# A 32-head softmax attention beside a linear attention on one core: the offset copies of the score tiles made by GpSimd alone, four tiles at a time

## The chip, the core and the metric

One core of a Trainium2 chip. Five engines run their own instruction lists and meet at semaphores: TensorE (PE), VectorE (DVE), ScalarE (ACT), GpSimd (POOL) and SyncE (SP, which issues most transfers). The metric is the device time of one execution in microseconds, the median of several.

## The reference

Two attention blocks over x of 2048 x 512, each with 32 heads of 16, side by side in the output. Block A is linear attention (cheap), block B is full softmax attention and sets the size of the work.

```python
def _A_ref(x, wqkv, wo):            # q, k, v: 32 heads of 16
    phi = lambda t: jnp.where(t > 0, t + 1, jnp.exp(t)) + 1e-6
    pq, pk = phi(q), phi(k)
    kv = jnp.einsum("bhsd,bhse->bhde", pk, v)
    z = jnp.einsum("bhsd->bhd", pk)
    num = jnp.einsum("bhqd,bhde->bhqe", pq, kv)
    den = jnp.einsum("bhqd,bhd->bhq", pq, z)[..., None] + 1e-6
    ...                             # num / den, heads joined, @ wo
def _B_ref(x, wqkv, wo):
    scores = jnp.einsum("bhqd,bhkd->bhqk", q, k) * scale
    p = _softmax(scores, axis=-1)
    o = jnp.einsum("bhqk,bhkd->bhqd", p, v)
    ...                             # heads joined, @ wo
return jnp.concatenate([a, b], axis=-1)
```

## The kernel before

**The work.** Block B is cut into 32 units (`NU`): four groups of eight heads, four stretches of 512 queries, and even or odd heads of the group. A unit has 64 score tiles of 128 keys x 512 queries, four heads side by side in the four row groups of the PE array, so there are 2048 score tiles in all. The scores come scaled by `ESC`, so that an exponential in base two can be made from their bits.

**Two ways to the exponential.** Some score tiles go to ACT: one exponential over two or three PSUM banks (line 1095, written to `PT`). The others, called D tiles here, go to DVE: it adds a constant and writes the sum as a 16-bit integer (line 970, `DI`), whose bits are read as a half-precision number, a rough exponential. To smooth it, two more copies of `DI` with 341 and 683 added to the integers are made (line 1166, `DJ`; these are the shifts), and all three are multiplied with V, scaled by 1, 0.797 and 0.633 (`VV`, with `SW`). So an ACT tile costs one product with V, a D tile three. The products (line 1224) add up in one PSUM bank (`pPV`), four row groups at once.

**PSUM.** Eight banks: one for `pPV`, five for ACT's tiles in two slots of three and two banks (`ABL = (3, 2)`, tensor `pS`), two for D tiles and for the projections and block A (`pD`). The third bank of slot 0 can be lent to the D side; the ACT fill is then two banks wide.

**Groups and rings.** D tiles are gathered in groups of `DG = 3` in one of `NDG = 6` buffers of `DI`; a full group is shifted twice, each time into the next of `NDJ = 8` buffers of `DJ`. A buffer of `DJ` is free again when PE has used its tiles. A unit's end: DVE transposes `pPV` to `OT` (line 1354), inverts the sums (`ZRA`), POOL multiplies (`XN`, line 1359), DVE transposes back to `ON`. POOL makes the scaled copies of V too (line 671), but the first eight are made by DVE.

**What sets the order.** A planner in the kernel's own code walks a model of the four engines with a duration for each instruction and picks, at each step, the candidate that can start first, with priorities. The order that it finds is fixed for each engine; on the chip the engines only wait for each other's semaphores, and each list runs strictly in order. `want_lend` (line 984) decides whether slot 0 is filled with two or three banks; `d_pick` (913) lets a new D tile in while the modelled backlogs of DVE and POOL are below `DBL` and `PBL`; `shift_cand` (1148) chooses between POOL and DVE for each shift (`LM` is how much later POOL must be before DVE is taken); `pv_cand` (1181) places the products, with a higher priority once `VHI` of them are outstanding; `fill_idle` puts matmuls without a use into idle PE time, by the share of PE time that was streamed lately. `SEEDS` shifts the due times of block A's and the projections' jobs.

Of the kernel before, what the change touches and what calls it, by code (L numbers as in the profile page):

```python
# [13 lines left out]
ALU = mybir.AluOpType  # L14
# [3 lines left out]
class _Op:  # L18
    __slots__ = ("idx", "lane", "fn", "pos", "waits", "sig", "count", "vc",
                 "name", "queue")  # L20


class Sched:
    ENGINES = ("pe", "act", "dve", "pool")

    def __init__(self):
        self.ops = []
        self.lane_ops = defaultdict(list)
        self.queue_ops = defaultdict(list)
        self.last_write = {}  # L30
        self.readers = defaultdict(list)
        self.clock = defaultdict(dict)
        self.acc_tag = {}
        self.n_dma_lanes = 0

# [4 lines left out]
    def add(self, lane, fn, reads=(), writes=(), name="", queue=None,  # L40
            extra_deps=(), accum=None, force_signal=False):
        if queue is None:
            queue = lane
            assert lane in self.ENGINES, lane
        op = _Op()
# [7 lines left out]
        op.sig = force_signal  # L53
        op.count = 0
# [188 lines left out]
def bass_concat_heads__linear_attn_block__softmax_full_mha__prompt_kernel(nc, A_x, A_wqkv, A_wo, B_x, B_wqkv, B_wo, out):  # L243
# [11 lines left out]
    DG = 3  # L255
    NDG = 6
    NDJ = 8
    UB = NT * 4
    PVB = 8
    PVW = 0.3  # L260
# [4 lines left out]
    LD = 1  # L265
    LB = 99.0
    PB5 = 3.0
# [3 lines left out]
    DLEAD = 0.8  # L271
    DBL = 4.0
    PBL = 7.5
    SHL = ("pool", "pool")
    LM = 5.0
    FU = 0.6
    SEEDS = (0, 195, 365, 131, 7, 89, 76, 286, 0, 222, 34, 197, 397, 382, 371)
    SEG = 45.0
    JIT = 6.0
    LATE = 0.2  # L280
    DBAL = 1
    CPRIO = 0.9
    VHI = 24
    LONE = 0.0
    XNT = 0.63
# [6 lines left out]
    JU = 0.55  # L292
# [18 lines left out]
    with es:  # L311
# [51 lines left out]
        DBANK = [bank(DB, i, ("D", i)) for i in range(ND)] + [bank(SCT, aoff[0] + ABL[0] - 1, ("S", 0, ABL[0] - 1))]  # L363
# [95 lines left out]

        def vis(eng, en_):  # L460
# [19 lines left out]
        class Job:  # L480
# [8 lines left out]
            def start_time(self):  # L489
# [3 lines left out]
                if T["pe"] >= rd - AE and streaming(T["pe"]) < JU:  # L493
# [19 lines left out]
            def go(self, i, end, bk, bi):  # L513
# [4 lines left out]
                push(eng2, end if eng2 == eng else vis(eng, end),  # L518
# [41 lines left out]
        def first_units():  # L560
            def mm(bk, kind, c0, n, o0):
                def f(e):
                    for cc in range(4):
                        ins = mm4(e, bk[0][:, bk[2] + o0:bk[2] + o0 + n], Wb[:, cc, kind * 512:kind * 512 + 128], xTb[:, cc, c0:c0 + n], cc == 0, cc == 3)
# [9 lines left out]
            mm(ka, 1, 0, 128, 0)  # L574
            mm(DBANK[0], 0, 0, 256, 0)
            mm(DBANK[1], 0, 256, 256, 0)
            mm(kb, 1, 128, 384, 0)
            km(ka, 0, 0, 128, kma_keys(0))
            qt(DBANK[0], "act", 0)
            qt(DBANK[1], "dve", 256)  # L580
# [68 lines left out]
        def v4_job(t4, Gp, lane="pool", **kw):  # L649
# [14 lines left out]
            for k in (1, 2):  # L664
                if VVP == 1 and lane == "dve":
# [5 lines left out]
                st.append((lane, 0.74 if lane == "dve" else VVT, f_op(lane, lambda e, k=k: e.tensor_scalar(  # L671
                    vv(k), vv(0), SW[k], 0.0, op0=ALU.mult, op1=ALU.add),
                    [("VV", t, sl, 0) for t in ts] + [("VV1", sl)], [("VV", t, sl, k) for t in ts])))
# [202 lines left out]
        dfree = [0.0] * ND + [None]  # L876
        held = {}
        lent = [False]
# [34 lines left out]
        def d_pick(at, used):  # L913

            bi = min((i for i in range(ND + 1) if dfree[i] is not None), key=lambda i: (dfree[i], i), default=None)
# [727 lines left out]
```

## Time and profile before

| | us |
|---|---|
| median of 3 runs | 683.81 (683.69 to 686.09) |
| the profiled execution | 684.12 |
| its span, first to last instruction | 682.4 |
| busy: ACT / PE / POOL / DVE | 669.0 / 653.9 / 622.1 / 582.6 |

The profiled execution lies 0.31 us above the median, and 1.72 us of it lie outside the span. In the rows, a group reads: line, engine, operation, what is written from what, shape, count, then busy time and the mean of one in ns, then the engine's idle time before them and what ended it. Lines that run on one engine without a gap overlap in their latencies, so the pace of a run of equal instructions (its length less one, over their number less one) says more than the mean of one. A clock of 1.00 is TensorE at full speed.

### The profile page before, as it was taken

What the parts mean: (1) busy time and instruction counts of PE and PEld (TensorE: products, weight loads), DVE (VectorE), ACT (ScalarE), POOL (GpSimd) and SP (SyncE); (2) the same over time, 40 slices, a digit from 0 to 9 for tenths busy, and PEclk for the clock granted to TensorE, in tenths of its full rate; (3) what the DMA queues carried; (4) which work ended last, traced back from release to release, by engine and by line L of the source; (5) the groups of instructions that cost most, each with busy time, mean ns of one, the idle gap of its engine ahead of it and who ended that gap; (6) DMA issues with size and microseconds to landing.
All of it is one profiled execution on the core that took longest, in us unless ns stands there. A gap on an engine that the chain in (4) does not pass through costs nothing.

```text
span 682.4 us, 19594 instructions
## 1 busy us (share of the span) xinstructions
PE 653.9 (96%) x8530; PEld 209.9 (31%) x8530; DVE 582.6 (85%) x937; ACT 669.0 (98%) x706; POOL 622.1 (91%) x470
## 2 busy tenths in 40 slices
PE   8999999999999999999999999999999999999997
PEld 4323333222323333332322233222332222322223
DVE  5878898999789988868999898888888998898983
ACT  5999999999999999999999999999999999999997
POOL 6698999999699999999999999999999999999894
PEclk9999999999999999999999998999999999999999
DMA  9400012011101201130111000111010110001111
GB/s 207 103 2 2 17 16 35 10 31 23 34 2 33 33 17 17 22 82 11 24 25 33 24 18 18 24 47 25 18 36 13 33 32 25 9 17 33 47 41 35
DMA packets 55418, 21.76 MB, mean 32 GB/s; under 512 B 45600, under 2 KB 55328, under 8 KB 55328
## 3 DMA queue, kind: packets, MB, share of 16 engines
q1 hardware_dynamic: 54128, 20.07, 13.4%
q8 instruction: 68, 1.11, 0.7%
q10 hardware_dynamic: 1200, 0.39, 0.2%
q14 instruction: 22, 0.18, 0.1%
HBM read 4.19 MB, written 4.19 MB: 12 GB/s over the span
## 4 chain that ended last, share of the span: by engine, by line
ACT 87%; POOL 7%; PE 3%; DVE 2%; DMA 1%; issue 0%; ACTq 0%
ACT PT L1095 85%; POOL DJ L1166 6%; ACT pD L683 1%; DVE DI L970 1%; PE pS L863 1%; DMA xTb<-in_B_x_dram 1%; ACT pS L683 1%; PE pD L535 1%; PE pPV L1224 1%; PE pS L535 1%; PE pS L654 0%; POOL XN L1359 0%; ACT KV L539 0%; POOL VV L671 0%; DVE DJ L1166 0%
## 5 line engine op out<-in xcount | busy, mean ns | idle before, releaser
L1095 ACT ACTIVATE PT<-pS 128x1024 f16<-128x1024 f32 (+1 forms) x666 | 660.5, 1353 | 2.6 <-PE pS L863 1.8
L1166 POOL TENSOR_SCALAR DJ<-DI 128x1536 int16<-128x1536 int16 (+1 forms) x391 | 579.5, 1483 | 48.0 <-DVE DI L970 21.6
L970 DVE TENSOR_SCALAR DI<-pD 128x512 uint16<-128x512 f32 (+1 forms) x456 | 315.2, 705 | 48.4 <-PE pD L863 42.8
L863 PE MATMUL pS<-QT,KM 32*128 32x512 bf16 x1573 | 261.5, 385 | 21.3 <-ACT PT L1095 15.0
L1224 PE MATMUL pPV<-PT,VV 128*17 128x512 f16 (+1 forms) x1420 | 244.0, 378 | 0.5 <-DVE OT L1354 0.5
L1224 PE MATMUL pPV<-DJ,VV 128*17 128x512 f16 (+1 forms) x1256 | 231.9, 379 | 0.7 <-POOL DJ L1166 0.5
L863 PE MATMUL pD<-QT,KM 32*128 32x512 bf16 x475 | 168.5, 385 | 0.3 <-DVE PQT L684 0.3
L863 PEld LDWEIGHTS pS<-QT,KM 32*128 32x128 bf16 x1573 | 64.3, 91 | 278.0 <-ACT PT L1095 260.3
L1224 PE MATMUL pPV<-DI,VV 128*17 128x512 f16 (+1 forms) x628 | 148.3, 379 | 0.5 <-DVE OT L1354 0.4
L970 DVE TENSOR_SCALAR DI<-pS 128x512 uint16<-128x512 f32 x153 | 104.1, 681 | 8.0 <-PE pS L863 4.4
L1224 PEld LDWEIGHTS pPV<-PT,VV 128*17 128x17 bf16 x1420 | 49.8, 88 | 44.0 <-issue 38.1
L1224 PEld LDWEIGHTS pPV<-DJ,VV 128*17 128x17 bf16 x1256 | 47.9, 88 | 47.2 <-issue 35.6
L863 PEld LDWEIGHTS pD<-QT,KM 32*128 32x128 bf16 x475 | 39.7, 91 | 9.3 <-issue 4.1
L1224 PEld LDWEIGHTS pPV<-DI,VV 128*17 128x17 bf16 x628 | 31.2, 88 | 22.4 <-issue 18.4
L1166 DVE TENSOR_SCALAR DJ<-DI 128x1536 int16<-128x1536 int16 x29 | 28.3, 977 | 0.0
L535 PE MATMUL pD<-xTb,Wb 128*32 128x512 bf16 (+1 forms) x368 | 26.7, 379 | 0.0
L535 PE MATMUL pD<-Wa,xTa 128*32 128x256 bf16 x672 | 26.4, 275 | 0.0
L1354 DVE STREAM_TRANSPOSE OT<-pPV 128x512 f32<-128x512 f32 x31 | 22.0, 708 | 0.7 <-PE pPV L1224 0.6
L1359 POOL TENSOR_TENSOR XN<-OT,ZRA 128x256 bf16<-128x256 f32 x31 | 19.5, 630 | 1.2
L683 ACT ACTIVATE pD<-pD 128x512 f32<-128x512 f32 x22 | 19.6, 893 | 0.0
L671 POOL TENSOR_SCALAR VV<-VV 128x544 bf16<-128x544 bf16 x24 | 17.3, 723 | 0.9
L535 PEld LDWEIGHTS pD<-Wa,xTa 128*32 128x32 bf16 x672 | 15.4, 96 | 8.7 <-issue 5.4
(109 smaller groups left out, 392.3 us busy)
## 6 DMA issues: line engine op xcount, KB each, us to landing
out_dram<-KV SPq DMA_DIRECT2D x31, 128.0 KB, 1.7
Wa<-in_A_wqkv_dram SPq DMA_DIRECT2D x3, 512.0 KB, 4.2
KM<-KR SPq DMA_DIRECT2D x96, 16.0 KB, 1.8
Wb<-in_B_wqkv_dram SPq DMA_DIRECT2D x2, 384.0 KB, 4.6
Wb<-in_B_wqkv_dram SPq DMA_DIRECT2D x1, 512.0 KB, 4.4
Wa<-in_A_wo_dram SPq DMA_DIRECT2D x1, 512.0 KB, 4.5
Wb<-in_B_wo_dram SPq DMA_DIRECT2D x1, 512.0 KB, 3.8
xTa<-in_A_x_dram SPq DMA_TRANSPOSE x24, 3.4
```

Source lines behind the costliest of these rows:

```text
L535: ins = e.matmul(out[32 * g:32 * g + 32], lhsT=lhsT[:, 32 * g:32 * g + 32], rhs=rhs, start=start, stop=stop, tile_position=(0, 32 * g))
L671: st.append((lane, 0.74 if lane == "dve" else VVT, f_op(lane, lambda e, k=k: e.tensor_scalar(vv(k), vv(0), SW[k], 0.0, op0=ALU.mult, op1=A ...
L683: ex = lambda bk: sch.add("act", lambda e: e.activation(x(bk), x(bk), ACTF.Exp), reads=[bk[3]], writes=[bk[3]])
L863: return e.matmul(dst, lhsT=KM[32 * g:32 * g + 32, Gp % 2, e_, j * 128:(j + 1) * 128], rhs=QT[32 * g:32 * g + 32, Gp % 2, c * 512:(c + 1) ...
L970: sch.add("dve", lambda e: e.tensor_scalar(DI.bitcast(U16)[:, buf, i * 512:(i + n) * 512], f32v(DBANK[bi], 512 * n), EB, IMAX, op0=ALU.add ...
L1095: sch.add("act", lambda e: e.activation(PT[:, row, c0:c0 + w], SCR[sl][:, 0:w], ACTF.Exp, scale=SC / ESC), reads=skeys(sl)[:len(bl)], writ ...
L1166: sch.add(ln, lambda e: e.tensor_scalar(J, I, 1.0, float(SH[k]), op0=ALU.mult, op1=ALU.add), reads=[("DI", buf, i) for i in range(n)], wri ...
L1224: sch.add("pe", lambda e: e.matmul(dst[32 * g:32 * g + 17, 0:n], lhsT=VV[:, Gp % 2, k, j, 17 * h:17 * h + 17], rhs=P[:, q0:q0 + n], start= ...
L1354: sch.add("dve", lambda e: e.transpose(OT[:, 0, :], PVb[:, 0:512]), reads=[("PV", g) for g in range(4)], writes=[("OT", 0)])
L1359: mul = f_op("pool" if XNP else "dve", lambda e: e.tensor_tensor(xn[:, :, 16 * e_:16 * e_ + 16], o[:, :, 0:16], zr.unsqueeze(2).broadcast_ ...
```

## The change

It touches the planner's numbers and some of its rules; the arithmetic of a tile stays.

- A group has four D tiles (`DG = 4`), in four `DI` buffers (`NDG = 4`) and six `DJ` buffers (`NDJ = 6`). A shift covers 128 x 2048.
- `LM = 99` keeps every shift on POOL. DVE's eight copies of V stay, but POOL's next instruction now waits for each of them (`hold`).
- `LD = 2` gives `want_lend` another rule: slot 0 is filled with two banks when jobs hold more D-side banks than are lent; with three when a D-side bank is free; else with two if a job is due or the backlogs are small. With `LDA` the rule also runs over the end of a unit.
- Five sets of planner constants (`MODES`) take turns by stretches of 45 us, chosen by `SEEDS`; jobs on POOL are modelled 0.8 us later (`JM`).
- The first projections are whole 128-wide matmuls instead of four 32-wide ones each.

```diff
-    DG = 3
-    NDG = 6
-    NDJ = 8
+    DG = 4
+    NDG = 4
+    NDJ = 6
...
-    LD = 1
-    LB = 99.0
-    PB5 = 3.0
+    LD = 2
+    LB = 2.0
+    PB5 = 9.0
...
-    LM = 5.0
+    LM = 99.0
...
-    SEEDS = (0, 195, 365, 131, 7, 89, 76, 286, 0, 222, 34, 197, 397, 382, 371)
+    SEEDS = (0, 2, 96, 277, 222, 0, 142, 42, 2, 142, 131, 32, 289, 309, 14)
...
-    VHI = 24
...
+    MODES = ((0.8, 36, 0.7, 0.2, 9.0), (1.2, 36, 0.7, 0.2, 9.0), (0.8, 48, 0.9, 0.2, 10.5), (1.2, 28, 0.7, 0.1, 9.0), (1.0, 36, 0.55, 0.35, 8.0))
+    LDA = 1
+    JM = 0.8
...
@@ Sched.add
+        if lane == "pool" and self.hold:
+            extra_deps = list(extra_deps) + self.hold
+            self.hold = []
...
@@ first_units
-                        ins = mm4(e, bk[0][:, bk[2] + o0:bk[2] + o0 + n], Wb[:, cc, kind * 512:kind * 512 + 128], xTb[:, cc, c0:c0 + n], cc == 0, cc == 3)
+                        ins = e.matmul(bk[0][:, bk[2]:bk[2] + n], lhsT=Wb[:, cc, kind * 512:kind * 512 + 128], rhs=xTb[:, cc, c0:c0 + n], start=(cc == 0), stop=(cc == 3))
...
@@ v4_job
+                if lane == "dve":
+                    def alone(bk, cp=cp):
+                        sch.hold.append(cp(bk))
+                        sch.hold[-1].x = 0.27
...
@@ d_pick
-            if bi is None or u is None or dfree[bi] > at or d_backlog(at) > DBL or p_backlog(at) > PBL or lagging(at):
+            if bi is None or u is None or dfree[bi] > at or d_backlog(at) > DBL or p_backlog(at) > mode()[4] or lagging(at):
...
@@ want_lend
-            if LD == 3:
+            if LD == 1:
                 return nh >= 1
...
+            free = sum(1 for x in dfree if x is not None and x <= t_ + 0.1)
+            if LD == 2 and sum(1 for i in range(len(dfree)) if held.get(i)) > sum(lent):
+                return True
+            if free:
                 return False
-            if nh >= 1 and LD != 2:
-                return True
...
-            return False
+            return d_backlog(t_) <= LB and p_backlog(t_) <= PB5
...
@@ shift_cand
-            dp, dd = POOLT(w), 0.40 + w * 0.0003
+            dp, dd = POOLT(w), DSH + max(0.0, T["pool"] - sd)
...
@@ pv_cand
-            pr = 1 if out_ >= VHI or final else 4
+            pr = 1 if out_ >= mode()[1] or final else 4
```

Three places show how the order moves. The names are those of the words above; a row is one run of equal instructions, in the order of the engine.

POOL from its first shift. Before:

```order
L1166 TENSOR_SCALAR DJ<-DI 128x1536 x14
L1359 TENSOR_TENSOR XN<-OT,ZRA 128x16x16
L1166 TENSOR_SCALAR DJ<-DI 128x1536 x11
L1359 TENSOR_TENSOR XN<-OT,ZRA 128x16x16
L1166 TENSOR_SCALAR DJ<-DI 128x1536 x6
L671 TENSOR_SCALAR VV<-VV 128x544 x4
```

POOL from its first shift, now:

```order
L1184 TENSOR_SCALAR DJ<-DI 128x2048 x10
L1379 TENSOR_TENSOR XN<-OT,ZRA 128x16x16
L1184 TENSOR_SCALAR DJ<-DI 128x2048 x8
L681 TENSOR_SCALAR VV<-VV 128x544 x5
L1184 TENSOR_SCALAR DJ<-DI 128x2048 x2
L1379 TENSOR_TENSOR XN<-OT,ZRA 128x16x16
```

Fewer and wider shifts stand between the ends of two units, and in the first units nearly as many tiles as before (40 shifted tiles instead of 42 up to the first `XN`, 40 instead of 33 up to the second).

PE from the first projections. Before:

```order
L535 MATMUL pS<-xTb,Wb 32x128 x16
L535 MATMUL pD<-xTb,Wb 32x256 x32
L535 MATMUL pS<-xTb,Wb 32x384 x16
L863 MATMUL pS<-QT,KM 128x512 x2
L535 MATMUL pD<-xTb,Wb 32x512 x16
L863 MATMUL pS<-QT,KM 128x512 x5
```

PE from the first projections, now:

```order
L573 MATMUL pS<-xTb,Wb 128x128 x4
L573 MATMUL pD<-xTb,Wb 128x256 x8
L573 MATMUL pS<-xTb,Wb 128x384 x4
L544 MATMUL pD<-xTb,Wb 32x512 x8
L881 MATMUL pS<-QT,KM 128x512 x2
L881 MATMUL pD<-QT,KM 128x512
L881 MATMUL pS<-QT,KM 128x512
L544 MATMUL pD<-xTb,Wb 32x512 x8
L881 MATMUL pS<-QT,KM 128x512 x4
```

The projection of the second stretch of keys, which stood in one piece behind the first score fill, now stands half ahead of it and half behind it, and two D tiles follow the first fill.

DVE at the end, from the last unit's first transpose. Before:

```order
L1288 STREAM_TRANSPOSE OT<-pPV 128x256
L1289 RECIPROCAL ZRA<-OT 128x8
L1288 STREAM_TRANSPOSE OT<-pD 128x256
L1289 RECIPROCAL ZRA<-OT 128x8
L1292 STREAM_TRANSPOSE ON<-XN 128x256
L1290 TENSOR_TENSOR XN<-OT,ZRA 128x8x16
L1292 STREAM_TRANSPOSE ON<-XN 128x256
L621 TENSOR_REDUCE ZRA<-ZRA 128x1 x2
L634 TENSOR_SCALAR BN<-ZRA 128x1
L635 SCALAR_TENSOR_TENSOR BN<-ZRA,BN 128x1
```

DVE at the end, now:

```order
L1309 STREAM_TRANSPOSE OT<-pPV 128x256
L1309 STREAM_TRANSPOSE OT<-pD 128x256
L1310 RECIPROCAL ZRA<-OT 128x8 x2
L1311 TENSOR_TENSOR XN<-OT,ZRA 128x8x16
L1313 STREAM_TRANSPOSE ON<-XN 128x256
L631 TENSOR_REDUCE ZRA<-ZRA 128x1 x2
L644 TENSOR_SCALAR BN<-ZRA 128x1
L645 SCALAR_TENSOR_TENSOR BN<-ZRA,BN 128x1
L1313 STREAM_TRANSPOSE ON<-XN 128x256
```

The second half of the last unit's queries now goes first, and the four small instructions of the range flag (`BN`) stand ahead of the other half's transpose to `ON`, which waits for POOL's `XN`.

Over the whole program: 314 shifts instead of 420 (391 on POOL and 29 on DVE before), 626 D tiles instead of 628, of which 125 instead of 153 in the lent bank, and ACT's exponentials are 519 of two banks and 127 of three instead of 579 and 86. Of the shifts on POOL, 88 name PE among what they wait for, instead of 27.

112 lines of the change are left out of this document (61 added, 51 removed).

## The prediction

> **What bounds the kernel now.** I read the page's busy shares and its chain first, then the groups by shape, then ACT and POOL in order of time, the clock in short stretches, and the tail.
>
> ```profile
> PE 653.9 (96%) x8530; PEld 209.9 (31%) x8530; DVE 582.6 (85%) x937; ACT 669.0 (98%) x706; POOL 622.1 (91%) x470
> ACT 87%; POOL 7%; PE 3%; DVE 2%; DMA 1%; issue 0%; ACTq 0%
> ```
>
> ACT is busy 98% of the span and carries 87% of the chain. ACT in order of time shows how little it stands still:
>
> ```profile
> 8.83 1.02 ACT L1095 ACTIVATE PT<-pS 128x1024 f16<-128x1024 f32 x1 [1.00 <-PE pS L863]
> 10.41 57.89 ACT L1095 ACTIVATE PT<-pS 128x1024 f16<-128x1024 f32 x56 [0.56 <-PE pS L863]
> ...
> 408.79 2.86 ACT L1095 ACTIVATE PT<-pS 128x1024 f16<-128x1024 f32 x3 [0.26 <-PE pS L863]
> ...
> 418.94 1.02 ACT L1095 ACTIVATE PT<-pS 128x1024 f16<-128x1024 f32 x1 [0.37 <-PE pD L863]
> 420.41 64.86 ACT L1095 ACTIVATE PT<-pS 128x1024 f16<-128x1024 f32 x65 [0.45 <-PE pD L863]
> ...
> 674.48 1.51 ACT L1016 ACTIVATE PT<-pS 128x768 f16<-128x768 f32 x2
> ```
>
> From its first exponential at 8.83 to the last one's end at 675.99 it waits only 0.56 us at the start and 0.26 + 0.37 + 0.45 = 1.08 us around 410 to 420. Behind it come 6.4 us of tail. So no order of these instructions can win more than about 1.6 us on ACT, unless ACT gets less to do.
>
> Where the 1.08 us come from, the chain and the clock tell:
>
> ```profile
> 347.11 1.47 POOL DJ L1166
> ...
> 406.29 1.48 POOL DJ L1166
> ```
>
> ```profile
> 414.00:416.00 2.00, 1.42 (x21) 0.72 (x20) 1.09 (x2) 2.00 (x3) 1.92 (x2) 1.00 0.00 0
> 416.00:418.00 2.00, 2.00 (x20) 0.89 (x19) 1.97 (x5) 2.00 (x3) 1.92 (x2) 0.70 0.00 0
> 418.00:420.00 2.00, 2.00 (x18) 1.07 (x15) 1.22 (x3) 1.59 (x2) 1.85 (x2) 0.50 0.00 0
> ```
>
> From 347 to 408 the chain runs mostly through POOL's shifts: POOL sets the pace there. Then PE is busy 1.42 us of 2 (first figure behind the length), its granted clock (third from the right) falls to 0.70 and 0.50, and ACT (fourth busy figure) loses 0.41 us in the last stretch. A late POOL is thus what already costs this kernel its only stall in the middle.
>
> The groups by shape that the change touches, and POOL's and DVE's shifts with shortest, middle and longest:
>
> ```profile
> L1166 POOL TENSOR_SCALAR DJ<-DI 128x1536 int16<-128x1536 int16 x389 | 578.2, 1488 | 47.8 <-DVE DI L970 21.6
> L1095 ACT ACTIVATE PT<-pS 128x1024 f16<-128x1024 f32 x579 | 574.9, 1299 | 2.6 <-PE pS L863 1.8 <-PE pD L863 0.8
> L970 DVE TENSOR_SCALAR DI<-pD 128x512 uint16<-128x512 f32 x437 | 292.1, 683 | 44.5 <-PE pD L863 38.9 <-PE pS L863 2.2
> L1095 ACT ACTIVATE PT<-pS 128x1536 f16<-128x1536 f32 x86 | 148.2, 1723 | 0.0
> L1166 DVE TENSOR_SCALAR DJ<-DI 128x1536 int16<-128x1536 int16 x29 | 28.3, 977 | 0.0
> L970 DVE TENSOR_SCALAR DI<-pD 128x1024 uint16<-128x1024 f32 x19 | 23.1, 1217 | 3.9 <-PE pD L863 3.9
> L1166 POOL TENSOR_SCALAR DJ<-DI 128x512 int16<-128x512 int16 x2 | 1.2, 618 | 0.2
> ```
>
> ```profile
> L1166 POOL TENSOR_SCALAR DJ<-DI x391: 618/1472/1893, 13.1 to 671.4; 128x1536 int16<-128x1536 int16 x195, 128x512 int16<-128x512 int16 x1
> ...
> L1166 DVE TENSOR_SCALAR DJ<-DI x29: 543/894/1598, 64.9 to 621.4; 128x1536 int16<-128x1536 int16 x29
> ```
>
> **The change part by part.** *ACT's work.* A two-bank exponential takes 0.92 us of ACT where they run densely (row below); one of three banks costs 1723 - 1299 = 424 ns more, 1.34. So 60 fewer of two and 41 more of three are -55.2 + 55.1, and one half-filled one goes: about -0.5 us. The last bank is not lent more but less (125 D tiles in it instead of 153), and that decides nothing by itself. Bound by ACT, the kernel can lose its 1.08 us and no more.
>
> ```profile
> 342.42 2.76 ACT PT L1095 x3
> ```
>
> *POOL's work* is the term that decides. POOL in order of time gives the pace of a shift and of what stands between:
>
> ```profile
> 339.36 15.42 POOL L1166 TENSOR_SCALAR DJ<-DI 128x1536 int16<-128x1536 int16 x10
> ...
> 38.34 1.47 POOL L1166 TENSOR_SCALAR DJ<-DI 128x1536 int16<-128x1536 int16 x1
> 39.78 0.62 POOL L1359 TENSOR_TENSOR XN<-OT,ZRA 128x256 bf16<-128x256 f32 x1
> 40.47 1.47 POOL L1166 TENSOR_SCALAR DJ<-DI 128x1536 int16<-128x1536 int16 x1
> ...
> 68.65 2.57 POOL L671 TENSOR_SCALAR VV<-VV 128x544 bf16<-128x544 bf16 x4
> ...
> 669.89 3.02 POOL L1166 TENSOR_SCALAR DJ<-DI 128x1536 int16<-128x1536 int16 x2 [0.21 <-DVE DI L970]
> ```
>
> ```profile
> L1359 POOL TENSOR_TENSOR XN<-OT,ZRA x31: 618/621/919, 39.8 to 662.5; 128x256 bf16<-128x256 f32 x31
> ```
>
> A shift of three tiles has a pace of (15.42 - 1.47) / 9 = 1.55 us. One of four isn't in the trace: by the line through 618 ns for one tile and 1472 for three, each further tile takes 427 ns, so 1.90 and with the same 0.08 between two, 1.98. The 618 rests on two instructions; if a lone tile took 0.70, the line would give 1.94; if nothing of a shift were fixed, 1.55 x 4/3 = 2.07. I take 1.98. An `XN` adds 40.47 - 38.34 - 1.55 = 0.58, a copy of V 2.57 / 4 = 0.64.
>
> Between the first and the last `XN` POOL now has 298 wide shifts, 30 `XN` and 24 copies: 590.0 + 17.4 + 15.4 = 622.8 us. Before, that stretch took 662.5 - 39.8 = 622.7 us, with 370 shifts x 1.55 + 32.8 = 606 us of work in it; the rest were waits and slowed shifts. So POOL, which had 16 us to spare, has none: it must not stand still once from 40 to 662 us to keep the pace of ACT. Behind the last `XN` it has 0.58 + 4 x 1.98 + 2 x 1.13 = 10.8 us, so its last shift ends at 39.8 + 622.8 + 10.8 = 673.4 at best. Before, it ended at 669.89 + 3.02 = 672.9, and its last products ran at 675.24 (row below), 2.3 us later. So 1.8 us of idle time in POOL are free; each further one moves the end.
>
> How much idle? Before, POOL waited 21.6 us for D tiles:
>
> ```profile
> POOL DJ L1166 <- DVE DI L970: 21.6, 16, 5.0
> ...
> 20.09 6.26 POOL L1166 TENSOR_SCALAR DJ<-DI 128x1536 int16<-128x1536 int16 x4 [0.85 <-DVE DI L970]
> 28.54 3.16 POOL L1166 TENSOR_SCALAR DJ<-DI 128x1536 int16<-128x1536 int16 x2 [2.19 <-DVE DI L970]
> 33.71 6.11 POOL L1166 TENSOR_SCALAR DJ<-DI 128x1536 int16<-128x1536 int16 x4 [2.00 <-DVE DI L970]
> ```
>
> 5.0 + 0.85 + 2.19 + 2.00 of them lie before 40 us, where the first `XN` waits for its unit anyway, so some 11.5 us lie behind. The planner now lets D tiles in until POOL is 9 instead of 7.5 us behind, and DVE has fewer other things to do, so less is left: between 0 and 11.5 I take a quarter, 3 us. That is 1.2 us beyond what is free.
>
> *DVE* loses 29 shifts (28.3 us) and gains 28 x 0.683 - 14 x 1.217 = 2.1 us for wide conversions taken apart. It has 2% of the chain: nothing on the path. *The shared way of the two.* POOL's shifts average 1488 against a middle of 1472: 389 x 16 ns = 6.2 us lost, which go with DVE's shifts; the 1.98 above is already free of them. The Trainium skill's page "SBUF — State Buffer" (section "SBUF: two separate sides") says that GpSimd and certain VectorE instructions hold a port pair for a whole instruction while the other blocks. By it 29 shifts of at least 543 ns would have cost POOL up to 15.7 us instead of 6.2; the sum takes the rows. *The eight `hold` waits* stand by the order ahead of the first `XN`, where POOL waits for D tiles already: 0. *PE* has the same score fills, four products fewer: 0. *SP's transfers* are the same and cost 1% of the chain: 0.
>
> *The start.* The projection that delayed the second exponential by 0.56 now stands half ahead of the first fill:
>
> ```profile
> 8.39 0.09 PEld L863 LDWEIGHTS pS<-QT,KM 32*128 32x128 bf16 x2 [0.32 <-DVE QT L571]
> ...
> 8.72 1.05 PE L535 MATMUL pD<-xTb,Wb 128*32 128x512 bf16 x16
> ```
>
> Its half, 0.53 us, fits partly into the 0.32 us that PE waits there. Between -0.56 and +0.5 I take -0.3 for ACT; where POOL sets the end it is worth nothing.
>
> *The tail.* DVE's end now runs the flag's small instructions ahead of the last transpose:
>
> ```profile
> 675.24 0.28 PE L1224 MATMUL pPV<-DJ,VV 128*17 128x256 f16 x2
> ...
> 677.87 0.45 DVE L1292 STREAM_TRANSPOSE ON<-XN 128x256 bf16<-128x256 bf16 x1
> 678.23 0.20 DVE L621 TENSOR_REDUCE ZRA<-ZRA 128x1 f32<-128x17 f32 x2
> ...
> 678.59 0.16 DVE L635 SCALAR_TENSOR_TENSOR BN<-ZRA,BN 128x1 f32<-128x1 f32 x1
> ```
>
> From 678.23 to 678.75 is 0.52 us, after which the last two output tiles follow: +0.6, between 0 and 1.
>
> Sum: 682.4 + 1.2 + 0.6 = 684.2 of span; 1.72 outside it make 685.9 against the profiled 684.12. The median lies 0.31 below that execution: **685.6**, 0.3% more than 683.81. By a measurement of this kernel, under 0.5% (3.4 us) can't be told from no change.
>
> **The rivals.** *A, POOL's growth is hidden.* POOL idles less than 1.8 us and ACT keeps the end, without the stall at 410 to 420: 682.4 - 1.1 - 0.5 - 0.3 + 0.6 = 681.1, at the median's level 682.5. For it: the deeper backlog and six `DJ` buffers of four tiles, as many tiles as eight of three. Against it: any 1% on a shift is 5.9 us.
>
> *B, the forecast*, POOL paces: 684 to 687.2 with 1.5 to 4.5 us of idle time.
>
> *C, slower: late shifts thin out PE's stream.* The place is wherever POOL falls behind, as at 414 us. One such event cost 1.08 us. POOL is now at its limit through all 32 units, not in one stretch of 60 us; two events on top of the forecast carry it past 687.2, four give 685.6 + 4.3 = 689.9. For it: more shifts wait for PE to empty a `DJ` buffer, the ring of which turns in 6 x 1.98 = 11.9 us instead of 12.4, and POOL's idle time there adds up. Against: in the trace of before POOL waits for PE nowhere. The Trainium skill's page "GPSIMD Engine Reference" (section 4.1, "Engine selection") speaks against the change in the same sense: elementwise work belongs on VectorE. The trace bears that out for one shift, 543 ns on DVE undisturbed against 1472.
>
> *D, faster by over 0.5%*: under 680.4 ACT would have to do less or start sooner than its rows allow.
>
> **How the numbers follow.** A 0.27, B 0.41, C 0.29, D 0.03. A and nearly all of B lie within 0.5%, with 0.05 of B above: faster 0.03, same 0.63, slower 0.34. The range reaches from A's middle into C, 682 to 692 (five events and an error of 1% in the shift); B's own is 684 to 687.2.
>
> **What would show it.** Shifts at 1.90 us with 0.08 between; POOL busy over 94% and its last shift's end between 673 and 677; POOL's share of the chain well over 7%; ACT's idle time near 3 us, in a few places behind PE's products that wait for `DJ`; the first exponentials without a gap of 0.5; the last `ON` behind the flag's rows. The prediction falls if a wide shift isn't near 1.98, if POOL waits long for PE or DVE, or if the clock drops repeatedly.

## The result, and the profile after

The changed kernel takes 686.99 us (median; 685.83 to 689.0), the kernel before beside it 684.14: a ratio of 1.0038, interval 1.0027 to 1.005. That lies in the range forecast (682 to 692), 1.4 us above the forecast of 685.6, and within the half per cent under which the prediction saw no change. The interval lies above 1 all the same: the changed kernel is the slower one, by about 0.4%. The forecast's sum, though, put the time in the wrong place.

The profiled execution has a span of 685.1 us against 682.4. The busy shares and the chain of the changed kernel:

```profile
PE 649.2 (95%) x8481; PEld 212.3 (31%) x8481; DVE 560.6 (82%) x920; ACT 668.5 (98%) x686; POOL 635.8 (93%) x393
ACT 82%; PE 10%; POOL 5%; DMA 1%; issue 0%; DVE 0%; ACTq 0%
```

POOL works longer and carries *less* of the chain (5% instead of 7%), PE 10% instead of 3%. POOL's share is a weak sign, since it varies with the execution: 0 to 6% in six traces of the changed lists, 7 to 15% in four of the lists of before (most of them come below). The groups by shape that the change touches:

```profile
L1184 POOL TENSOR_SCALAR DJ<-DI 128x2048 int16<-128x2048 int16 x312 | 593.1, 1901 | 36.7 <-DVE DI L988 12.3 <-DVE VV L681 2.1
L1111 ACT ACTIVATE PT<-pS 128x1024 f16<-128x1024 f32 x519 | 530.1, 1263 | 3.7 <-PE pS L881 1.9 <-PE pD L881 1.6
L1111 ACT ACTIVATE PT<-pS 128x1536 f16<-128x1536 f32 x127 | 212.9, 1677 | 0.5 <-PE pS L881 0.5
```

A wide shift takes 1901 ns, and POOL's list in order of time gives the pace, (5.86 - 1.90) / 2 = 1.98:

```profile
658.61 5.86 POOL L1184 TENSOR_SCALAR DJ<-DI 128x2048 int16<-128x2048 int16 x3
```

ACT in order of time, every place where it stands still and its end:

```profile
8.93 16.19 ACT L1111 ACTIVATE PT<-pS 128x1024 f16<-128x1024 f32 x17 [1.60 <-PE pS L881]
25.39 9.27 ACT L1111 ACTIVATE PT<-pS 128x1024 f16<-128x1024 f32 x10 [0.28 <-PE pS L881]
35.48 14.71 ACT L1111 ACTIVATE PT<-pS 128x1024 f16<-128x1024 f32 x15 [0.82 <-PE pD L881]
...
533.62 5.54 ACT L1111 ACTIVATE PT<-pS 128x1024 f16<-128x1024 f32 x5 [0.28 <-PE pD L881]
...
562.62 1.02 ACT L1111 ACTIVATE PT<-pS 128x1024 f16<-128x1024 f32 x1 [0.48 <-PE pD L881]
564.14 110.95 ACT L1111 ACTIVATE PT<-pS 128x1536 f16<-128x1536 f32 x108 [0.49 <-PE pS L881]
674.67 1.83 ACT L1031 ACTIVATE PT<-pS 128x768 f16<-128x768 f32 x2
679.25 0.60 ACT L548 ACTIVATE KV<-pS 128x512 bf16<-128x512 f32 x1 [2.76 <-PE pS L544]
679.88 0.39 ACTq L1333 DMA_DIRECT2D out_dram<-KV  x1
680.37 0.60 ACT L548 ACTIVATE KV<-pD 128x512 bf16<-128x512 f32 x1 [0.52 <-PE pS L544]
680.87 0.59 ACT L548 ACTIVATE KV<-pS 128x512 bf16<-128x512 f32 x1
```

The first row is the start, the last five the tail. Cut at the first exponential and at the last one's end, the two executions compare like this:

| us | before | after |
|---|---|---|
| first exponential starts | 8.83 | 8.93 |
| from there to the last one's end | 667.16 | 667.57 |
| of it, ACT stands still | 1.64 | 2.35 |
| behind the last exponential | 6.4 | 8.6 |

So 2.2 of the 2.7 us lie behind the last exponential. In the middle the gap of 0.56 us at the start is gone, as expected, but 1.10 us come in at 25 and 35 us. There PE is the bound: it now makes four projections between 20 and 36 us, where the kernel before had one. PE's projection matmuls from 20 to 36 us, first after the change, then before it:

```profile
L544 PE MATMUL pS<-xTb,Wb 128*32 128x512 bf16 x48 | 3.7, 384 | 0.0
...
L544 PE MATMUL pD<-xTb,Wb 128*32 128x512 bf16 x16 | 1.0, 379 | 0.0
```

```profile
L535 PE MATMUL pD<-xTb,Wb 128*32 128x512 bf16 x16 | 1.2, 384 | 0.0
```

In stretches of four microseconds (behind the length: busy time of PE, weight loads, DVE, ACT and POOL, then the granted clock), after the change and before it:

```profile
24.00:28.00 4.00, 4.00 (x60) 2.29 (x50) 3.86 (x6) 3.73 (x5) 3.76 (x2) 1.00 0.02 4
32.00:36.00 4.00, 4.00 (x60) 1.35 (x64) 3.81 (x7) 3.18 (x4) 3.18 (x2) 1.00 0.02 4
```

```profile
24.00:28.00 4.00, 3.63 (x40) 1.52 (x38) 2.47 (x5) 4.00 (x5) 2.28 (x2) 1.00 0.00 0
32.00:36.00 4.00, 3.97 (x42) 0.93 (x42) 3.60 (x4) 4.00 (x5) 2.21 (x2) 1.00 0.01 2
```

PE is busy without a break at a clock of 1.00, and ACT stands still. Around 562 us the granted clock is down to 0.50, as it was around 418 before: one event of 0.97 us in place of one of 0.82 (0.37 + 0.45; the 0.26 that the prediction counted in lies at 408.8, 8 us ahead of the drop). The middle as a whole is no slower than before, though: three further traces of the lists of before, shown below, take 667.0 to 668.1 us from first to last exponential.

The tail. DVE's last instructions after the change:

```profile
676.40 0.45 DVE L1309 STREAM_TRANSPOSE OT<-pPV 128x256 f32<-128x256 f32 x1 [6.02 <-PE pPV L1245]
676.88 0.45 DVE L1309 STREAM_TRANSPOSE OT<-pD 128x256 f32<-128x256 f32 x1
...
678.09 0.45 DVE L1313 STREAM_TRANSPOSE ON<-XN 128x256 bf16<-128x256 bf16 x1
678.46 0.20 DVE L631 TENSOR_REDUCE ZRA<-ZRA 128x1 f32<-128x17 f32 x2
...
678.88 0.44 DVE L1313 STREAM_TRANSPOSE ON<-XN 128x256 bf16<-128x256 bf16 x1
```

The flag's rows stand ahead of the last `ON`, as forecast. What the forecast missed is that the two halves of the last unit have changed places: the half that DVE multiplies itself is first, because the half that POOL multiplies is modelled 0.8 us later. Its output tiles are then copied first too, and one of them is stored by ACT, in front of ACT's two remaining copies (the rows at 679.88 to 680.87 above; before, ACT's copies ran in one piece and its store was last). The issue of the last store ends 5.3 us behind the last exponential instead of 4.2, and the stores land later. The stores of the last four tiles, before and after, from issue to landing:

```profile
DMA to landing us min/median/max: 1.7/1.9/2.1
```

```profile
DMA to landing us min/median/max: 2.5/2.8/2.9
```

### The profile page after: what moved, and what is told of

Read it like the earlier page. It is cut to its first block, busy times and chain, and to the rows that moved or that the text cites. A ratio compares the mean times of both kernels' runs of the same rounds, so it can differ in the third digit from the quotient of the medians.

```text
span 685.1 us, 19434 instructions
## 1 busy us (share of the span) xinstructions
PE 649.2 (95%) x8481; PEld 212.3 (31%) x8481; DVE 560.6 (82%) x920; ACT 668.5 (98%) x686; POOL 635.8 (93%) x393
## 3 DMA queue, kind: packets, MB, share of 16 engines
q8 instruction: 68, 1.11, 0.7%
## 4 chain that ended last, share of the span: by engine, by line
ACT 82%; PE 10%; POOL 5%; DMA 1%; issue 0%; DVE 0%; ACTq 0%
ACT PT L1111 80%; POOL DJ L1184 5%; PE pS L881 3%; PE pPV L1245 3%; ACT pD L701 2%; PE pD L544 1%; PE pS L544 1%; DMA xTb<-in_B_x_dram 1%; PE pD L1245 0%; PE pD L664 0%; ACT pS L701 0%; PE pD L881 0%; POOL XN L1379 0%; PE pS L573 0%; PE pD L573 0%
## 5 line engine op out<-in xcount | busy, mean ns | idle before, releaser
L1184 POOL TENSOR_SCALAR DJ<-DI 128x2048 int16<-128x2048 int16 x314 | 595.2, 1895 | 36.9 <-DVE DI L988 12.3
L988 DVE TENSOR_SCALAR DI<-pD 128x512 uint16<-128x512 f32 (+1 forms) x496 | 334.6, 689 | 64.3 <-PE pD L881 54.4
L881 PE MATMUL pS<-QT,KM 32*128 32x512 bf16 x1547 | 254.9, 386 | 25.3 <-ACT PT L1111 18.2
L1245 PE MATMUL pPV<-PT,VV 128*17 128x512 f16 (+1 forms) x1422 | 231.4, 380 | 0.0
L1245 PE MATMUL pPV<-DJ,VV 128*17 128x512 f16 (+1 forms) x1252 | 222.3, 380 | 2.4 <-POOL DJ L1184 1.4
L881 PE MATMUL pD<-QT,KM 32*128 32x512 bf16 x501 | 183.0, 385 | 0.2 <-DVE KV L548 0.2
L988 DVE TENSOR_SCALAR DI<-pS 128x512 uint16<-128x512 f32 x125 | 85.3, 682 | 8.1 <-PE pS L881 4.7
L548 DVE CAST KV<-pD 128x512 bf16<-128x512 f32 x26 | 17.8, 685 | 7.7 <-PE pD L544 7.7
L544 PE MATMUL pD<-xTb,Wb 128*32 128x512 bf16 x320 | 23.7, 383 | 0.0
L544 PE MATMUL pD<-Wa,KV 128*32 128x512 bf16 x256 | 19.7, 384 | 0.0
```

Of the source, the lines that this page charges most:

```text
L544: ins = e.matmul(out[32 * g:32 * g + 32], lhsT=lhsT[:, 32 * g:32 * g + 32], rhs=rhs, start=start, stop=stop, tile_position=(0, 32 * g))
L548: return lambda e, bk: (e.tensor_copy(out_fn(), in_fn(bk)) if lane == "dve" else e.activation(out_fn(), in_fn(bk), ACTF.Copy))
L881: return e.matmul(dst, lhsT=KM[32 * g:32 * g + 32, Gp % 2, e_, j * 128:(j + 1) * 128], rhs=QT[32 * g:32 * g + 32, Gp % 2, c * 512:(c + 1) ...
L988: sch.add("dve", lambda e: e.tensor_scalar(DI.bitcast(U16)[:, buf, i * 512:(i + n) * 512], f32v(DBANK[bi], 512 * n), EB, IMAX, op0=ALU.add ...
L1184: op = sch.add(ln, lambda e: e.tensor_scalar(J, I, 1.0, float(SH[k]), op0=ALU.mult, op1=ALU.add), reads=[("DI", buf, i) for i in range(n)] ...
L1245: sch.add("pe", lambda e: e.matmul(dst[32 * g:32 * g + 17, 0:n], lhsT=VV[:, Gp % 2, k, j, 17 * h:17 * h + 17], rhs=P[:, q0:q0 + n], start= ...
```

## Experiments on POOL's pace

The theory after this reading: the time is ACT's list, a start in which PE is the bound, and the tail. The rival is the forecast's own: POOL's pace sets the end.

**POOL made faster**, all lists unchanged but for one fill by DVE at the start:

```diff
+        sch.add("dve", lambda e: e.memset(DJ[:, :, 1536:2048], 12000), writes=[("DJ", i) for i in range(NDJ)])
...
-                op = sch.add(ln, lambda e: e.tensor_scalar(J, I, 1.0, float(SH[k]), op0=ALU.mult, op1=ALU.add),
+                wp = min(w, 1536)
+                op = sch.add(ln, lambda e: e.tensor_scalar(J[:, 0:wp], I[:, 0:wp], 1.0, float(SH[k]), op0=ALU.mult, op1=ALU.add),
```

> The changed kernel with its lists as they are, but each four-tile shift writes only the first 1536 of its 2048 columns (the last quarter of each DJ buffer holds a constant, so a part of the smoothing copies is left out). POOL's work falls by some 312 x 0.43 = 134 us, to about 500. Theory 'ACT's list': the time is ACT's work, the start where PE is the bound, and the tail, so at most the stalls in the middle go (0.3 + 1.0 us): 685.5 to 686.8. Rival 'POOL paces': POOL sets the end through all 32 units, and with its load gone the end of the last exponential comes 2 us or more sooner: 685 or less.

Measured: 686.22 us, 1.0036 (1.0023 to 1.0049). POOL's share falls from 93% to 73% and it leaves the chain:

```profile
PE 649.4 (95%) x8481; PEld 212.4 (31%) x8481; DVE 561.1 (82%) x921; ACT 668.1 (97%) x686; POOL 502.2 (73%) x393
ACT 88%; PE 9%; DMA 1%; DVE 0%; ACTq 0%; issue 0%
```

From first to last exponential it takes 666.9 us; the six traces with the changed lists and full shifts (the changed kernel itself and five variants of its tail below) take 666.5 to 667.6. So 134 us less work on POOL win nothing that can be told apart: POOL's pace is not what the changed kernel pays. The stalls stay as well. Those at 25 and 35 us are 0.28 and 0.81 here (2 us later, as the first exponential is), and the clock is down around 562 us again. The stretch from 560 to 570 us, after the change and with the faster POOL (columns as above):

```profile
560.00:570.00 10.00, 10.00 (x102) 2.05 (x102) 6.79 (x13) 8.86 (x10) 9.66 (x6) 0.73 0.11 16
```

```profile
560.00:570.00 10.00, 9.99 (x98) 2.41 (x99) 6.99 (x12) 8.72 (x9) 6.08 (x6) 0.69 0.08 16
```

PE's waits ahead of the event name ACT, and no shift, in both traces (553 to 560 us), and in the kernel before too (410 to 417 us):

```profile
PE pS L881 <- ACT PT L1111: 1.0, 4, 0.3
```

```profile
PE pS L882 <- ACT PT L1112: 1.0, 4, 0.3
```

```profile
PE pS L863 <- ACT PT L1095: 0.6, 2, 0.3
```

So that event is not a late POOL's. It stands in all nine traces of the changed lists and comes with them; what in the order of PE's list makes it isn't shown. Nor is a late POOL shown as the cause of the event in the kernel before: the prediction read it from POOL's part in the chain up to 408 us.

**POOL made slower**, in two doses, lists unchanged. First a tiny fill:

```diff
+        SLOW = sb("SLOW", [128, 1], F32)
...
+                def shift(e, slow=(jn[0] % 8 == 0)):
+                    if slow:
+                        e.memset(SLOW[:], 0.0)
+                    return e.tensor_scalar(J, I, 1.0, float(SH[k]), op0=ALU.mult, op1=ALU.add)
-                op = sch.add(ln, lambda e: e.tensor_scalar(J, I, 1.0, float(SH[k]), op0=ALU.mult, op1=ALU.add),
+                op = sch.add(ln, shift,
```

> The changed kernel with its lists as they are, and one tiny fill of 128x1 put on POOL ahead of every eighth shift: about 40 more instructions of some 0.1 to 0.15 us, 4 to 6 us of POOL's time, spread over the whole run. Theory 'ACT's list', with POOL's slack small: POOL was idle 1.5 us behind its first XN, and 1.3 us late at the end by ACT's measure, so 1 to 3 us come through: 688 to 690. Rival 'POOL paces all the time': the whole 4 to 6 us come through, 691 to 693. Rival 'POOL is hidden': 687.0. If late shifts thin out PE's stream, the granted clock falls in some places and the time grows by more than what was added.

Measured: 687.1 us, 1.0047 (1.0032 to 1.0061), no different from the changed kernel. The dose was too small to decide: of the 39 fills of 98 ns 33 stand between two shifts, and all but one of these (0.19) moved the next shift by 0.03 or 0.04 us. POOL's last shift, counted from the first exponential, ends 0.3 us later. So a larger one: `SLOW` 128 x 512, ahead of every sixteenth shift.

> The changed kernel with a fill of 128x512 float32 on POOL ahead of every sixteenth shift, 20 in all, of 0.5 us or somewhat more each: 10 to 12 us more work for POOL, spread over the run (the tiny fills of the run before it took 0.1 us each and moved POOL's last shift by only 0.3 us). POOL was idle 1.5 us behind its first XN, and 1.8 us at its end are free. If POOL has no other spare time, 7 to 9 us come through: 694 to 696. If ACT's list hides more (deep backlogs of D tiles, POOL's share of the chain only 5%), less: under 690. If the late shifts thin out PE's stream, ACT's stalls come with a granted clock of 0.5 in several places, and the time goes past 697.

Measured: 696.12 us, 1.0179 (1.0165 to 1.0194); there were 19 fills:

```profile
L1187 POOL MEMSET SLOW<- 128x512 f32 x19 | 10.0, 525 | 0.8
...
ACT 50%; POOL 33%; PE 13%; issue 2%; DVE 2%; DMA 1%; ACTq 0%
```

Of 10.0 us of fills 9.1 come through (696.12 - 686.99; from first to last exponential it is 676.2 against 667.1), and POOL now has a third of the chain. The 15 fills that stand between two shifts moved the next by 0.46 us each, not by their 525 ns, so by estimate all 19 add 8.8 us to POOL's list; its last shift, counted from the first exponential, ends 9.4 us later. So POOL and ACT are balanced to about 1 us: more POOL work costs its full price, less wins nothing. Here the forecast's rival C can be seen too. The same ten microseconds in the slowed kernel and in the changed one:

```profile
120.00:125.00 5.00, 3.65 (x24) 0.80 (x24) 3.91 (x8) 4.47 (x5) 4.87 (x4) 0.84 0.00 0
125.00:130.00 5.00, 5.00 (x44) 0.97 (x40) 1.99 (x4) 3.53 (x4) 4.77 (x5) 0.50 0.04 11
```

```profile
120.00:125.00 5.00, 4.37 (x45) 1.06 (x44) 4.81 (x10) 5.00 (x7) 4.84 (x3) 1.00 0.01 2
125.00:130.00 5.00, 4.90 (x84) 1.86 (x88) 2.97 (x5) 5.00 (x6) 4.77 (x5) 1.00 0.09 23
```

A fill stands in POOL's list at 120.72, and PE waits for the shift behind it (waits of PE from 120 to 126 us, slowed kernel):

```profile
PE pPV L1250 <- POOL DJ L1188: 1.2, 2, 0.9
```

PE is busy 3.65 us of 5, the clock falls to 0.50, PE is then the bound, and ACT loses 0.53 + 1.47 = 2.0 us of ten where it lost none. POOL itself stands still for 2.2 us behind its first `XN`, against 1.5 in the changed kernel, so this event makes up 0.7 of the 9.1 us at most.

**GpSimd makes all the shifts, alone:**

```diff
-    LM = 5.0
+    LM = 99.0
```

in the kernel before, groups still three wide.

> The kernel before with one number of the change: VectorE makes no shifts (LM = 99); groups stay three wide and all other rules as they were. By the list GpSimd makes all of 1186 D tile copies in three-wide shifts, and the planner lets in 593 D tiles instead of 628, so ACT gets 505 exponentials of two banks and 148 of three instead of 579 and 86: 505 x 0.92 + 148 x 1.344 - 579 x 0.92 - 86 x 1.344 = 15.2 us more. Theory 'ACT's list': 684 + 15 = 699, within 1.5. Rival 'POOL can do it as it stands': under 690. Rival 'late shifts make it worse still': over 702.

Measured: 698.6 us, 1.0221 (1.0203 to 1.0239), near the 699 of the theory of ACT's list:

```profile
PE 651.9 (94%) x8463; PEld 212.5 (30%) x8463; DVE 541.2 (78%) x873; ACT 682.1 (98%) x693; POOL 622.5 (89%) x475
ACT 96%; PE 1%; DVE 1%; DMA 1%; ACTq 0%; issue 0%
```

POOL isn't overloaded here. The planner lets in fewer D tiles, and ACT gets the rest. The theory's 15.2 us were met in part by luck: from first to last exponential this kernel takes 12.1 us more than the one before (679.3 against 667.2), and 2.8 more come behind the last exponential, where its two halves have changed places as well. What the rest of the change brings back is the D tiles: 628 before, 593 with this part alone, 626 in the whole. The four-wide groups were not tried without the other rules.

## Experiments on the tail

**The extra 0.8 us not applied in the last half unit**, so that both `ON` transposes stand ahead of the flag's rows:

```diff
-                push(eng2, end if eng2 == eng else vis(eng, end) + (JM if eng == "pool" else 0.0),
+                push(eng2, end if eng2 == eng else vis(eng, end) + (JM if eng == "pool" and lopen[0] else 0.0),
```

> The changed kernel (687.0 us, 1.0038 of the kernel before), with the extra 0.8 us on modelled POOL jobs dropped in the last half unit alone; the lists are the same up to there, and behind it DVE's two last transposes stand next to each other again, ahead of the flag's small instructions. Theory 'tail': the last ON is written 0.5 us sooner, 2.3 instead of 2.8 us behind the last exponential's end, and the time falls by 0.4 to 0.5, to 686.5. Rival 'POOL paces': the end is set by POOL's last shift, so the last exponential's end and all before it stay, and nothing is won beyond those 0.5; if the stores land late whatever stands ahead of them, nothing is won at all.

Measured: 686.72 us, 1.0041 (1.0025 to 1.0056): 0.3 us less than the changed kernel, nothing that can be told from no change. The last `ON` ends 2.36 us behind the last exponential instead of 2.82, but ACT's first copy still starts 2.76 behind it, since it waits for the products of the half that is first. ACT's last copy ends at 4.95 against 4.96. The forecast's +0.6 for the flag's rows was a price for something that the end does not wait for.

**ACT's store moved to SP:**

```diff
-                                          reads=kst(tl), queue="act" if tl == 3 else "sp", force_signal=True))
+                                          reads=kst(tl), queue="sp", force_signal=True))
```

> The changed kernel with the store of one of the last four output tiles issued by SP instead of ACT, so that it no longer stands between ACT's work and ACT's last two copies. Theory 'tail': those copies start 0.4 to 0.5 us sooner and the time falls by as much, to 686.5; the landing stays at 2.5 to 2.9 us. Rival: the issue by ACT costs nothing, since the copies wait for PE's products anyway: 687.0, and with four stores in a row on SP perhaps 0.3 more.

Measured: 687.02 us, 1.0043 (1.0031 to 1.0056). The copies did end 0.55 us sooner (4.41 us behind the last exponential instead of 4.96), but SP's four issues took 2.53 us, one of them 1.18 instead of 0.33, and gave it back.

**The whole order of the tail, undone in the changed kernel and done in the kernel before.** In the changed kernel the line above (`lopen[0]`), and:

```diff
+            if h == 0:
+                a, b = st[0][2], st[1][2]
+                st[0:2] = [("dve", 0.62, lambda bk: (a(bk), b(bk)))]
-            urgent.append(Job(st, [("ot", u - 1)], [(3, ("onf", h))] ...
+            urgent.append(Job(st, [("ot", u - 1)], [(len(st) - 1, ("onf", h))] ...
```

> The changed kernel up to the last exponential, and behind it the order of the kernel before: POOL jobs of the last half unit are modelled without the extra 0.8 us, and the first transpose and its reciprocal are one step. So the half that POOL multiplies is first again, its two output tiles are copied first, ACT's own store stands behind all of ACT's copies. Theory 'tail': of the 3.0 us between the kernels 2.2 to 2.5 lie behind the last exponential (6.4 us before, 8.1 to 9.2 in five traces of the changed order). The first copy comes 0.5 sooner, the last store is issued 1.2 sooner, and its landing falls from 2.5 to 3 us back to about 2: 684.5 to 685.0. Rival 'late landing has another cause' (its stores meet transfers of instructions whatever the order): only the 1.2 come back, 685.8. Rival 'the middle': POOL's or PE's pace makes the difference, and the tail gives 0.5 at most: 686.5.

Measured: 687.06 us, 1.0042 (1.0028 to 1.0056). No gain at all. In the kernel before:

```diff
-                push(eng2, end if eng2 == eng else vis(eng, end),
+                push(eng2, end if eng2 == eng else vis(eng, end) + (0.8 if eng == "pool" and not lopen[0] else 0.0),
```

> The kernel before with one thing of the change: POOL jobs of the last half unit are modelled 0.8 us later. Its lists are the same up to the last exponential; behind it the two halves change places, the half that DVE multiplies comes first, and ACT's store stands between its copies, as in the changed kernel. Theory 'tail': the stretch behind the last exponential grows from 6.4 to 8 us or more, the time from 683.9 to 685.5 to 686.2. Rival 'late landing has another cause': the last store is issued 1.2 us later and lands as fast as before: 685.1. Rival 'the middle': no more than 684.4.

Measured: 685.79 us, 1.0031 (1.0019 to 1.0043): the swap alone costs the kernel before 2.1 us by the medians, and 0.8 by its trace. The profiled execution was the fastest of six (684.61), so what the others add can't be read. And one more look at the kernel before, for the spread:

> The kernel before once more, for a second trace of it: in five traces of the changed order the first exponential starts at 8.9 to 9.3 us in three, and at 10.9 and 11.1 in two, where the first products ran at half pace; the stores land in 2.5 to 2.8 us (medians). If the start and the landings vary in the same way with the run and not with the order, this trace shows it: a first exponential at 8.8 or near 11, landings of 1.7 to 2.1 us if they belong to the order, up to 2.8 if they belong to the run.

Measured: 684.85 us, first exponential at 8.76, landings of 1.7 to 2.1 us. The table puts these traces side by side, in us behind the last exponential's end; the last column is the rest behind the last store's issue.

| | last copy ends | last store's issue ends | the end | rest |
|---|---|---|---|---|
| before, both traces | 3.8 | 4.2 | 6.4 | 2.2 |
| before, halves swapped | 5.0 | 5.3 | 7.2 | 1.9 |
| after | 5.0 | 5.3 | 8.6 | 3.3 |
| after, order of before | 3.9 | 4.7 | 9.3 | 4.6 |

In the kernel before the swap costs 1.2 us up to the last store's issue, and 0.8 of it reach the end: this part of the tail theory holds. Undone in the changed kernel, the copies end 1.1 us sooner, the last store's issue 0.6, and the run still ends no sooner. So something else holds the changed kernel's end, behind its last store. The records of the engines' own instructions say where it lies. After the tail each engine reads the flag and jumps over a fallback that isn't used; the columns are the start of ACT's jump, the start of the next instruction that ACT has, and the difference:

```
before                  680.98   681.46   0.48
before, second trace    681.66   682.14   0.48
before, halves swapped  680.72   681.20   0.48
after                   681.40   684.38   2.98
after, order of before  683.80   687.60   3.80
```

In the last of these, ACT's jump is what ends the run (687.60 of 687.9). PE's jump is longer as well, 0.8 to 1.7 us in eight of the nine traces of the changed lists and 0.5 in one, against 0.5 in all four of those before; the group of the jumps of the changed kernel, and that of the kernel before with its halves swapped:

```profile
L1609 PEldq COMPARE_BRANCH  x1: 1498/1498/1498, 680.9 to 680.9; - x1
```

```profile
L1587 PEldq COMPARE_BRANCH  x1: 497/497/497, 680.8 to 680.8; - x1
```

**Is it the code behind the jump?** Both kernels give PE, DVE and ACT a hint that the jump will be taken, 60 entries ahead of the end (`HINT`). The Trainium skill's page "Runtime: NRT & Kernel Launch" (section "Instruction fetch mechanics") says that a jump to code that isn't loaded waits for a transfer, and that code comes in blocks of 256 instructions. The profile of the changed kernel agrees on the size: one queue has 1.11 MB in 68 loads, so 16 KB each, as many as PE's 17,100 instructions need. The theory was that on ACT a new block begins between hint and jump, and the hint's load is lost. It was tried in three kernels. The order of before in the tail, and a later hint on ACT:

```diff
-                           mark=(HINT, lambda e: loc.append(e.mark_branch_hint_location())) if queue in HQ else None)
+                           mark=(40 if queue == "act" else HINT, lambda e: loc.append(e.mark_branch_hint_location())) if queue in HQ else None)
```

> The changed kernel with the last half unit in the order of the kernel before, and ACT's hint that the jump behind the flag will be taken given 40 instead of 60 entries ahead of the end of ACT's list. In the run with that order alone, ACT's jump (from 683.80) needed 3.8 us, against 0.48 in all three traces of the kernel before, and it ended last; in all six others of the changed order it needed 2.7 to 3.8. Theory 'code': the hint's load is lost on the way (67 ACT instructions lie between hint and jump, and a block of code begins among them in the changed kernel, not in the one before); with a later hint the jump takes 0.5 again, the loads of code no longer meet the stores, and the stretch behind the last exponential falls from 9.3 to 6.4 to 7.2 us: 684.5 to 685.2. Rival 'only the jump': the stores stay late (2.1 to 2.6 us), and 685.5 is left. Rival 'the jump's length has nothing to do with the hint's place': 687.0.

The later hint alone:

> The changed kernel with ACT's hint 40 instead of 60 entries ahead of its end, and nothing else: all lists keep their order. Theory 'code': ACT's jump takes 0.5 instead of 3.0 us; POOL, which waits for the stores, still ends the run, and it gains only what the stores win when ACT's two loads of code no longer run beside them: 0.4 to 0.9, 686.1 to 686.6. Rival 'the jump's length has nothing to do with the hint's place': ACT's jump stays at 2.7 to 3.8, 687.0.

And the kernel before with `100 if queue == "act"`:

> The kernel before with ACT's hint 100 instead of 60 entries ahead of its end, so that by the count of instructions a block of code begins between hint and jump here too. Theory 'code': ACT's jump, 0.48 us before, takes 2.7 to 3.8; it starts at about 681.0, so ACT's end moves from 681.5 to 683.7 to 684.8, behind that of POOL (682.1), and the time goes from 683.8 to between 685.3 and 686.5. Rival: the jump stays at 0.5 and the time at 683.8.

Measured: 687.51 us, 1.0053 (1.0039 to 1.0068); 686.5 us, 1.0034 (1.0022 to 1.0046); 683.96 us, 1.0003 (0.999 to 1.0016). ACT's jump took 3.04, 2.92 and 0.48 us. The hint's place makes no difference in any of them, so this theory of the hint falls, and with it the hope to mend the tail. That the jump waits for code fits the traces, but isn't shown: in all ten with a long jump of ACT, loads of instructions start between the jump and ACT's next instruction, and in the four with 0.48 us none does. With the order of before the first of the three again ended its copies early (3.9 us behind the last exponential), and its last stores were late instead:

```profile
L1336 SPq DMA_DIRECT2D out_dram<-KV x3: 332/463/1343, 678.6 to 680.5; - x3
...
DMA to landing us min/median/max: 2.0/2.8/3.1
```

What the traces show is a regularity without a cause. All four traces of the kernel before's lists up to the tail have ACT's jump at 0.48 us, landings of 1.7 to 2.1 and 1.9 to 2.2 us behind the last store. All nine of the changed kernel's lists have the jump at 2.7 to 3.8, median landings of 2.1 to 2.8 and 2.6 to 4.6 us behind the last store. The kernel before with `LM = 99` has 3.4 us for ACT's jump and 3.8 us behind the last store, so the wide groups aren't needed for it. Moreover, in all nine of the changed lists a 16 KB load of PE's code starts within 0.4 us of the first of the last stores (in the profiled execution both at 679.88), in the four of before 2.3 to 2.7 us ahead of it (676.39 against 678.79 in the first). That load isn't needed for a late end either: with `LM = 99` the nearest one starts 3.0 us behind the first of the last stores, whose landings have a median of 1.9 us and a longest of 3.5. Whether such loads delay the stores, and why the jump's code is there in one program and not in the other, stays open; a kernel with the same lists but a few more instructions on PE and ACT, which would shift the blocks, wasn't tried.

## Why the prediction was right, and where its sum was wrong

- *ACT's work, -0.5 us.* Right. From first to last exponential less the stalls it is 665.2 against 665.5; over six traces of the changed lists and four of those before, the whole stretch averages 667.1 against 667.5.
- *A wide shift 1.98 us.* Right, 1.90 each and 1.98 from one to the next. The shared way costs nothing any more, as the step had it: the longest shift takes 1903 ns against a middle of 1901.
- *POOL has no spare, +1.2 us.* The step that failed, by its consequence. The balance is right, as 9.1 of 10.0 us that come through show: about 1 us to spare, where the forecast had up to 1.8 us of idle time free. But the idle time behind the first `XN` was 0.32 + 1.17 = 1.5 us and not 3, the last shift ended at 675.2 instead of 676.4, and a faster POOL wins nothing. It is rival A's mechanism, with a tail that A didn't have and with 2.35 us of stalls where A had them gone; that the time falls into B's 684 to 687.2 is not B's merit. In the span the sum missed by 0.9 us (685.1 against 684.2): 0.7 too much ahead of the last exponential's end, 1.6 too little behind it. That two misses cancel in part is luck.
- *The `hold` waits, DVE, SP: nothing.* Right. POOL waited 2.1 us for DVE's copies of V, all ahead of the first `XN`; DVE has 0% of the chain.
- *PE: nothing.* Wrong. Four projections between 20 and 36 us make PE the bound there, +1.10 us. The step counted PE's instructions and not where they stand; the order of PE's list up to 36 us shows it. The middle as a whole did not grow by it, as the averages above say.
- *The start, -0.3.* The gap of 0.56 went as said, and 1.10 us came in 15 and 25 us later.
- *The tail, +0.6.* The step that was mis-sized: +2.2 in the profiled pair. The row on which it rested, the flag's instructions, costs nothing. The swap of the halves costs 1.2 up to the last store's issue, which stands in the order of ACT's list (a copy, a store, two copies); the rest lies behind the last store and couldn't be read from any row of before; its cause stays open.
- *Rival C.* Its mechanism exists, and one event behind a late shift cost ACT 2.0 us when POOL was slowed, but in the changed kernel there is one event, as before, and POOL isn't its cause. The stall from which the rival took its price isn't shown to be one of these. *What would show it* was right on the shifts, the last shift's end, the first exponentials and the last `ON`; wrong on POOL's busy share (93%, not over 94%), on its share of the chain (5%, not well over 7%) and on ACT's idle time behind `DJ`.

## What to carry to other kernels

When an engine that is not the bound gets more work, ask for its balance and then test both sides: slow it and speed it up with the order kept. Here 134 us less won nothing, and some 9 us more cost 9. Look, too, at what a new order does at the two ends of the run: read the order of the *last* instructions of every queue, and then measure, since copies that ended half a microsecond or a whole one sooner won nothing here. Differences of a few tenths of a per cent can sit behind the last store, where no step of the kernel's own accounting looks.

## What the hardware showed that was not expected

The jump at the program's end took ACT 0.48 us in one kernel, 2.7 to 3.8 in another and 3.4 in a third, with the same source behind it, and the hint's place had no influence. A fill of 98 ns between two shifts on POOL moved the next one by 0.03 to 0.04 us, one of 525 ns by 0.46.

The start comes in two forms. In four of nine traces of the changed lists PE's first matmuls ran at about half pace and the first exponential started at 10.9 to 11.2 us instead of 8.9 to 9.5; in the five traces with the start of the kernel before it started at 8.3 to 8.8. PE's first rows, after the change and in the run with the faster POOL:

```profile
6.07 0.40 PE L573 MATMUL pS<-xTb,Wb 128*128 128x128 bf16 x4 [0.45 <-DMA xTb<-in_B_x_dram]
6.30 1.04 PE L573 MATMUL pD<-xTb,Wb 128*128 128x256 bf16 x8
```

```profile
6.45 0.61 PE L574 MATMUL pS<-xTb,Wb 128*128 128x128 bf16 x4 [0.83 <-DMA xTb<-in_B_x_dram]
6.85 1.92 PE L574 MATMUL pD<-xTb,Wb 128*128 128x256 bf16 x8
```

The second is the same list, and eight matmuls take 1.92 us instead of 1.04. The wait for the input ahead of them was 0.69 to 0.95 us in the four, but also up to 1.12 in others, so its length alone doesn't decide. The traces' record of the granted clock begins, with 1.00, at 9.8 to 10.4 us in the four and at 4.3 to 7.3 us in the ten others, which fits a full clock that came later. Whether the change made this start more frequent, or chance did, is open; it costs about 2 us where it occurs. The profiled execution of the changed kernel is not one of these and lies at the median (686.94), so the 1.4 us above the forecast don't need it.
